# State read placed beside M of chunks 2 and 3: one change of TensorE's tiling less per batch

## The chip, the cores and the metric

One core of one Trainium2 chip. The time is device microseconds of one execution, from runs on the chip; the span is what the profile of the same execution shows from the first to the last instruction (1.7 to 2.1 us less in most runs, up to 3.0 in a few).

## The reference

A cross attention between tokens and a small state, in both directions, followed by a feed-forward layer over all rows of its result:

```python
B, H, S, Ns, D = (8, 8, 512, 32, 64)           # x: (B,H,S,D), state: (B,H,Ns,D)
a  = softmax(scale * x @ state.T);   xread = a  @ state
a2 = softmax(scale * state @ x.T);   sread = a2 @ x
attn = concatenate([xread, sread], axis=2)     # -> rows (B*(S+Ns), H*D = 512)
h = attn @ w_in                                # w_in: (512, 2048)
return (h / (1 + exp(-1.702 * h))) @ w_out     # w_out: (2048, 512)
```

(Shortened: the maxima and the 1e-9 of the softmax are left out.) All in 32-bit floats.

## The kernel before

The matmuls here write to PSUM, in banks; the program copies a bank out before it is written again. The token rows never form `xread`: the kernel multiplies the state into `w_in` first. That product is called M, per batch, in four chunks of 512 columns; `up` then multiplies M by the softmax weights. The state read `sread` is formed for all batches and goes through the layer at the end. `down` (the product with `w_out`) and, from batch 2 on, `up` use a Strassen scheme (fewer products of blocks, paid for with sums of blocks), hence the sums of M, which VectorE adds.

Each instruction of TensorE carries a size in the trace, 128*128 or smaller, called its tiling: eight matmuls of M, of tiling 64*32, start within 47 ns (360.820 to 360.867 us) and the next eight 453 ns after the first of them, while full-size matmuls of 128*128 start 216 ns apart. An "excursion" below is a way out of the full tiling and back. Three tilings occur: 128*128 for all large products and transposes, 64*32 for scores and M, 128*32 for the state read:

```python
psA = ctx.enter_context(tc.tile_pool(name="psA", bufs=2, space=bass.MemoryType.PSUM))  # tag "att"
psH = ctx.enter_context(tc.tile_pool(name="psH", bufs=2, space=bass.MemoryType.PSUM))  # tag "h"
...
def by_state(b, ps, rhs):                      # scores and M: 64 rows, 32 columns
    for j in range(NPR):
        for g in range(NG):
            rows, st = slice(D * g, D * (g + 1)), slice(Ns * j, Ns * (j + 1))
            nc.tensor.matmul(ps[g][st], A[b]["stT"][rows, st], rhs(rows, j), start=True, stop=True)

def att_M(b, c, spare=False):                  # two PSUM banks, from psH if spare, else psA
    ...
    by_state(b, ps, lambda rows, j: w_in[c][rows, j])
    for g in range(NG):
        nc.scalar.copy(m[:, g], ps[g])

def att_eT(b, g):                              # turns the states' softmax weights (128*128)
    ps = att_ps([P, SCH, P], f"eT_{b}_{g}")    # one bank of psA
    ...
    nc.scalar.copy(a["eT"][:, g], ps)

def att_sread(b):                              # 128 rows, 32 columns
    ps = att_ps([P, NG, D], f"sr_{b}")         # one bank of psA
    ...                                        # 32 matmuls of 64 columns
    nc.scalar.copy(sr, ps.rearrange("p g d -> p (g d)"))
```

Batches 2 to 7 are prepared while the batch ahead goes through `down`: after each block of eight large matmuls `product` runs what is in the next of 14 slots. The blocks are named by their PSUM bank: x in slots 0, 1, 4, 5; y in 2, 3, 6, 7, 10, 11; z in 8, 9, 12, 13.

```python
        at(5, att_scores, b)
        at(5, att_M, b, 0)
        at(5, att_M, b, 1, True)
        ...                                    # softmax in both directions, VectorE and ScalarE
        at(8, att_M, b, 2)
        at(8, att_M, b, 3, True)
        at(9, up_sums, b, 0)
        for g in range(NG):
            at(9 + g, att_eT, b, g)
        at(11, att_sread, b)
        at(11, up_sums, b, 1)
        at(12, att_srT, b)
        at(12, up_sums, b, 2)
```

A 32-bit matmul is two instructions in the trace and a transpose one (the four of an eT slot are x4), so a block of eight is 16, a chunk of M 16 and the state read 64.

Of the kernel before, what the change touches and what calls it, by code (L numbers as in the profile page):

```python
# [20 lines left out]
def kernel(  # L21
# [362 lines left out]
    def att_slots(b):  # L384

        slots = [[] for _ in range(14)]

        def at(i, fn, *args):
            slots[i].append((fn, args))

        at(0, att_state, b)
        for j in range(NPR):
            at(j, att_xT, b, j)
# [4 lines that stand above are left out]
        at(5, att_blocks, b)  # L398
        at(5, att_s_max, b)
        at(5, att_s_exp, b)  # L400
        at(5, att_x_exp, b)
        at(5, att_s_norm, b)
        at(5, att_x_norm, b)
        at(8, att_M, b, 2)
        at(8, att_M, b, 3, True)
        at(9, up_sums, b, 0)
        for g in range(NG):
            at(9 + g, att_eT, b, g)
        at(11, att_sread, b)
        at(11, up_sums, b, 1)  # L410
        at(12, att_srT, b)
        at(12, up_sums, b, 2)
        return slots

# [338 lines left out]
    for b in range(1, B):  # L753
        ahead = b + 1 < B
        if not ahead:
            for f in range(NF):
                up_s(f)
                if f > HF and f % 2:
                    s12("sr", (f - HF) // 2, B * Ns)
                    s3("sr", (f - HF) // 2, B * Ns)  # L760
            strassen("sr", B * Ns, lambda r, n: out_s[nb * r.start : nb * r.stop, :, n])
        slots = att_slots(b + 1) if ahead else [[]]
        if b > 1:
            slots[0].insert(0, (up_strassen(b), ()))
        strassen(b, S, lambda r, n: out_x[b, r, :, n].rearrange("r q n -> q r n"), slots)
        if b + 2 < B:
            load_state(b + 2)
            load_x(b + 2)
# [30 lines left out]
```

## Time and profile before

| | before |
|---|---|
| time, median of the first 3 runs | 756.31 us (755.9 to 757.17) |
| span of the profiled run | 755.7 us |
| TensorE busy | 743.6 us, 98% |
| one pass (from one batch's first transpose, stT, to the next one's) | 81.612 us |
| tilings entered in a pass | scores with M 0 and 1; M 2 and 3; state read |

The pass is what to look at. There are six, so five distances between them, and these agree within 3 ns. The prediction shows the chain of work and the weight loads of the third pass.

### The profile page before, as it was taken

To read this page: it belongs to the slowest core of one execution; us is meant where nothing else is said; L and a number is where in the kernel's file an instruction comes from. 1 tells how busy PE (TensorE), PEld (TensorE's weight loads), DVE (VectorE), ACT (ScalarE), POOL (GpSimd) and SP (SyncE) were. 2 spreads that over 40 slices of the span, in tenths; PEclk is the share of its full clock that TensorE was granted. 3 is DMA by queue.
4 is the path that set the end of the run, shared out by engine and by line. 5 is a ranking of instruction groups with operands and counts; after the bars stand their busy time and mean duration, and the time that the engine had idled before them with its cause. 6 is when DMAs were issued, how large, how long until landed. Compare 5 with 4: busy or idle time off the path is not lost.

```text
span 755.7 us, 9853 instructions
## 1 busy us (share of the span) xinstructions
PE 743.6 (98%) x4171; PEld 563.8 (75%) x4171; DVE 413.9 (55%) x712; ACT 231.7 (31%) x411; POOL 0.8 (0%) x8
## 2 busy tenths in 40 slices
PE   8989999999999999999999999999999999999997
PEld 3423454467888878887788788887888778888886
DVE  5999699632646373555637264638364550225511
ACT  4667611022324241433134232424142312104200
POOL 0000000000000000000000000000000000000000
PEclk9999999999999999999999999999999999999999
DMA  9811245010030000300030003000130000000001
GB/s 233 330 61 52 84 152 159 0 57 1 28 78 10 1 15 29 74 1 15 29 74 0 1 29 87 3 1 15 38 64 1 15 29 15 0 22 8 0 15 42
DMA packets 48763, 35.22 MB, mean 47 GB/s; under 512 B 36432, under 2 KB 44112, under 8 KB 48720
## 3 DMA queue, kind: packets, MB, share of 16 engines
q1 hardware_dynamic: 48720, 34.61, 15.9%
q8 instruction: 32, 0.52, 0.3%
q14 instruction: 11, 0.09, 0.0%
HBM read 25.69 MB, written 8.91 MB: 46 GB/s over the span
## 4 chain that ended last, share of the span: by engine, by line
PE 96%; SPq 2%; ACT 1%; DMA 1%; issue 0%; DVE 0%; ACTq 0%
PE y L494 19%; PE z L494 13%; PE x L494 13%; PE upy L578 8%; PE h L422 8%; PE o L447 7%; PE upx L578 5%; PE upz L578 5%; PE M L276 4%; PE h_sr L422 4%; PE xT L258 2%; PE y_sr L494 1%; SPq L131 1%; PE sr L371 1%; PE s L276 1%; PE z_sr L494 1%
## 5 line engine op out<-in xcount | busy, mean ns | idle before, releaser
L494 PE MATMUL x<-w_out,g 128*128 128x256 f32 x448 | 100.2, 379 | 0.0
L494 PEld LDWEIGHTS x<-w_out,g 128*128 128x128 f32 x448 | 84.2, 190 | 11.4 <-ACT osb L454 0.2
L587 DVE TENSOR_TENSOR g<-upy,g 128x512 f32<-128x512 f32 x72 | 48.1, 689 | 68.7 <-PE upy L578 68.7
L584 ACT ACTIVATE g<-g 128x512 f32<-128x512 f32 x72 | 44.8, 630 | 84.8 <-DVE g L587 84.8
L422 PE MATMUL h<-aT,M 128*128 128x512 f32 x128 | 59.9, 614 | 4.4 <-ACT M L351 4.4
L351 ACT COPY M<-M 128x512 f32<-128x512 f32 x64 | 33.2, 596 | 95.1 <-PE M L276 95.1
L422 PEld LDWEIGHTS h<-aT,M 128*128 128x128 f32 x128 | 24.2, 194 | 37.9 <-issue 25.5
L494 PE MATMUL z<-sums,later 128*128 128x256 f32 x224 | 51.1, 382 | 0.0
L494 PE MATMUL z<-w_out,g 128*128 128x256 f32 x224 | 50.8, 382 | 0.0
L494 PE MATMUL y<-sums,later 128*128 128x256 f32 x224 | 50.5, 379 | 0.0
L494 PE MATMUL y<-sums,g 128*128 128x256 f32 x224 | 50.5, 379 | 0.0
L494 PE MATMUL y<-w_out,g 128*128 128x256 f32 x224 | 50.1, 382 | 0.0
L494 PEld LDWEIGHTS y<-w_out,g 128*128 128x128 f32 x224 | 42.1, 190 | 10.5 <-issue 5.0
L494 PEld LDWEIGHTS z<-sums,later 128*128 128x128 f32 x224 | 42.1, 190 | 10.5 <-issue 5.0
L578 PE MATMUL upx<-aT,M 128*128 128x256 f32 x192 | 49.3, 379 | 0.0
L578 PE MATMUL upy<-ta,M 128*128 128x256 f32 x192 | 49.3, 379 | 0.0
L494 PEld LDWEIGHTS z<-w_out,g 128*128 128x128 f32 x224 | 41.6, 190 | 6.2
L494 PEld LDWEIGHTS y<-sums,g 128*128 128x128 f32 x224 | 41.6, 190 | 5.2
L494 PEld LDWEIGHTS y<-sums,later 128*128 128x128 f32 x224 | 41.6, 190 | 5.2
L471 DVE TENSOR_TENSOR later<-g,g 128x512 f32<-128x512 f32 (+1 forms) x32 | 20.8, 651 | 40.7 <-ACT g L425 40.7
L511 DVE TENSOR_TENSOR osb<-z,later 128x512 f32<-128x512 f32 x14 | 9.7, 692 | 60.2 <-PE z L494 60.2
L578 PEld LDWEIGHTS upx<-aT,M 128*128 128x128 f32 x192 | 36.5, 190 | 5.0
(130 smaller groups left out, 1023.0 us busy)
## 6 DMA issues: line engine op xcount, KB each, us to landing
later<-in_moe_w_out_dram SPq DMA_DIRECT2D x16, 512.0 KB
out_dram<-osb SPq DMA_DIRECT2D x32, 256.0 KB
xn<-in_x_dram SPq DMA_DIRECT2D x28, 256.0 KB
w_out<-in_moe_w_in_dram SPq DMA_DIRECT2D x12, 512.0 KB
later<-in_moe_w_in_dram SPq DMA_DIRECT2D x4, 512.0 KB
sums<-in_x_dram SPq DMA_DIRECT2D x4, 256.0 KB
stn<-in_state_dram SPq DMA_DIRECT2D x16, 32.0 KB
out_dram<-osb_sr SPq DMA_DIRECT2D x4, 128.0 KB
```

Source lines behind the costliest of these rows:

```text
L131: nc.sync.dma_start(xn[b][:, c], x_v[b, c])
L258: nc.tensor.transpose(ps[:, c], x_heads(b, c, j), ident)
L276: nc.tensor.matmul(ps[g][st], A[b]["stT"][rows, st], rhs(rows, j), start=True, stop=True)
L351: nc.scalar.copy(m[:, g], ps[g])
L422: nc.tensor.matmul(hps, lhs[i], rhs[i], start=(i == 0), stop=(i == n - 1))
L447: nc.tensor.matmul(ops, G[key, f // 2][:, f % 2, P * r : P * (r + 1)], w_out[:, f], start=(f == 0), stop=(f == NF - 1))
L471: nc.vector.tensor_tensor(out=s1, in0=a21, in1=a22, op=ALU.add)
L494: nc.tensor.matmul(ps[:, r], lhs[f][:, P * r : P * (r + 1)], rhs[:, f], start=(first and r == 0 and f == 0), stop=(f == HF - 1), skip_grou ...
L511: nc.vector.tensor_tensor(out=o, in0=ps, in1=with_, op=ALU.add)
L578: nc.tensor.matmul(ps[:, k], lhs[:, o : o + P], rhs, start=(first and k == 0), stop=True, skip_group_check=True)
L584: nc.scalar.activation(out=dst, in_=src, func=AF.Gelu_apprx_sigmoid)
L587: nc.vector.tensor_tensor(out=dst, in0=ps, in1=x, op=ALU.add)
```

## The change

The intent: sr (128*32) goes to the same slot as M of chunks 2 and 3 (64*32), so that TensorE leaves the full tiling twice in a pass and not three times. For that the weights must be turned earlier (slot 8), and M 2 and 3 go from slot 8 to 9, chunk 3 first. The whole diff:

```diff
-        at(8, att_M, b, 2)
-        at(8, att_M, b, 3, True)
-        at(9, up_sums, b, 0)
         for g in range(NG):
-            at(9 + g, att_eT, b, g)
-        at(11, att_sread, b)
+            at(8, att_eT, b, g)
+        at(9, att_sread, b)
+        at(9, att_M, b, 3, True)
+        at(9, att_M, b, 2)
+        at(10, up_sums, b, 0)
         at(11, up_sums, b, 1)
-        at(12, att_srT, b)
+        at(11, att_srT, b)
         at(12, up_sums, b, 2)
```

## The prediction

What no trace or run of this case shows is cut out of the recorded text, and the cuts are marked. The sum came to 686 ns a pass before and 491 after, a gain of 195 ns. What its terms were, in starts of single records: 92 = 308-216 into M, 23 = 453-430 in M's first group, 134 = 564-430 out of M, 104 = 320-216 in the first z matmul; for sr 93, 24 = 80-56, 112 = 168-56 and 104. What TensorE does in these nanoseconds is not shown. The 136 ns for the step from sr to M were an estimate from two of them, 112 out of sr and 24 for a small first group. The two rivals about tiling: before the runs no trace ruled either out. That weights are loaded beside a running matmul is shown inside a block: a z load starts 2 ns after the matmul before its own (363.020 and 363.018 us).

> **What bounds the kernel now.** I read the page's engine shares first, then the chain of work that ended last, then that chain again in a window of one batch, then the timelines of TensorE's matmuls and weight loads in that window, and last ScalarE and VectorE there, for the margins.
>
> The page says that TensorE is the bound and that nearly nothing interrupts it:
>
> ```profile
> PE 743.6 (98%) x4171; PEld 563.8 (75%) x4171; DVE 413.9 (55%) x712; ACT 231.7 (31%) x411; POOL 0.8 (0%) x8
> ...
> PE 96%; SPq 2%; ACT 1%; DMA 1%; issue 0%; DVE 0%; ACTq 0%
> ```
>
> So a nanosecond that TensorE gives back is a nanosecond of the kernel, and work on VectorE (55%) or ScalarE (31%) that only moves costs nothing unless TensorE comes to wait for it. The other TensorE figure, the weight loads, is 75%: they too have room.
>
> The change touches batches 2 to 7, which are prepared in slots between the blocks of matmuls of the batch ahead; six passes, all alike. Here is the chain (start us, us, what) over the middle of the third pass:
>
> ```profile
> 347.60 1.02 PE s L276 x16
> 348.62 1.72 PE M L276 x32
> 350.33 7.11 PE y L494 x32
> 357.44 3.45 PE z L494 x16
> 360.89 1.88 PE M L276 x32
> 362.77 3.65 PE z L494 x16
> 366.42 0.44 PE eT L360 x4
> 366.86 3.46 PE y L494 x16
> 370.31 0.44 PE eT L360 x4
> 370.75 3.46 PE y L494 x16
> 374.20 1.03 PE sr L371 x64
> 375.23 3.65 PE z L494 x16
> 378.88 0.11 PE srT L381
> 378.99 3.46 PE z L494 x16
> ```
>
> Each piece begins where the one before ends: TensorE alone, no wait. What the reader should see is that pieces of equal work differ. Sixteen full-size matmuls take 3.45 or 3.46 us, also beside transposes, but 3.65 after M and after sr. The 32 instructions of M take 1.72 us right after the scores (same tiling) but 1.88 us between full-size matmuls. These 0.16 and 0.20 us are the price of going into a tiling and coming back. The weight loads of the same stretch show where it lies (start, us, and in brackets the idle time before):
>
> ```profile
> 360.82 0.18 PEld L276 LDWEIGHTS M<-w_in,stT 64*32 64x32 f32 x16 [0.33 <-issue]
> ...
> 362.70 3.32 PEld L494 LDWEIGHTS z<-sums,later 128*128 128x128 f32 x16 [0.84 <-issue]
> ...
> 374.13 0.94 PEld L371 LDWEIGHTS sr<-xn,eT 128*32 128x32 f32 x64 [0.33 <-issue]
> 375.16 3.32 PEld L494 LDWEIGHTS z<-w_out,g 128*128 128x128 f32 x16
> ```
>
> Idle with no releaser ("issue") is 0.33 us before each first load of a new tiling: no semaphore explains it. Note also the tilings: M is 64*32, sr is 128*32, the rest 128*128. They are three, not two.
>
> [...]
>
> **The change, part by part.**
>
> *One change less, and its size.* From starts of single records, third pass. Into M: the last full matmul starts at 360.511, the first M load at 360.819, that is 308 ns later where a full matmul streams 216[...]; the first group of eight M matmuls then takes 453 ns to the second instead of 430, so 23 ns[...]. Out of M: last group at 362.132, first z load at 362.696, 564 ns less 430 is 134; the first z matmul then takes 320 ns to the second instead of 216, another 104[...]. Sum 92+23+134+104 = 353 ns, as the chain had it (0.16+0.20).
> For sr: into it 93, its first group of four 80 instead of 56 ns, so 24; out of it 168 less 56 is 112, then 104. Sum 333 ns.
> Before, these two excursions cost 353+333 = 686 ns in each pass. After, sr, M of chunk 3 and M of chunk 2 follow one another in one slot: in 93+24, from 128*32 to 64*32 once, out 134+104. No run before has that step from one small tiling to the other, so its price is my choice. [...] Sum 117+136+238 = 491 ns. **Gain 686-491 = 195 ns a pass**; in the chain's terms one return to full size (0.20 us) goes and both ways into small tilings stay.
>
> *Transposes of the states' weights.* Eight eT instructions leave two slots of four and stand together in slot 8. They are 109 ns apart and the blocks beside them are 3.45 to 3.46 either way: at most 5 ns, call it nothing.
>
> *Work moved.* The number of matmuls, loads, copies and VectorE operations is the same: the diff only moves calls. Sums of M (up_sums) and srT move by a slot on engines with room.
>
> *Sum.* 6 passes x 0.195 = 1.17 us. A pass is now 81.61 us (M begins at 279.28 and at 360.89) and should be 81.41. The tail, batches 0 and 1 and the output are untouched. 756.31 - 1.2 = **755.1 us**, -0.16%.
>
> **Will a new wait take its place?** Each margin, from the third pass:
> The weights e2 must be normalized before the transposes, now in slot 8 at 360.9. VectorE ends the last of these (L316) at 355.06+0.48 = 355.5. Margin 5.3 us; the other passes show the same to 0.1.
> eT must be copied (0.58 us each, L361) before sr: two copies end some 1.1 us after the transposes, and a block of 3.45 us lies between. Margin over 2 us.
> PSUM: the pool of two banks that eT, sr and M of chunk 2 share goes round. M of chunk 2's second bank is the one sr was in, so it waits for the copy of sr. That copy starts 0.29 us after the last sr group (375.015 to 375.30) and takes 0.27, so some 0.6 us. In between stands M of chunk 3, in the other pool: 0.14 us of change, then 0.45+0.43 us. Its bank is wanted after about 1.0 us. Margin 0.4 us, the thinnest; this is plainly why chunk 3 goes first.
> The sums need all four M copies (0.48 us apart, L351): done about 2.3 us after M, and the first product that needs a sum comes four blocks and more later. VectorE has about 4 us of sums (L554 to L556) and was idle 3.71 us just before them, waiting for the second eT transpose. That wait goes. It is off TensorE's path either way.
>
> **The rivals.**
> *The step between the small tilings is free.* [...] Then the pass gains 195+136 = 0.33 us, the whole 2.0 us: 754.3. For it: nothing in the trace. [...]
> *The step costs as much as going out and back in,*[...]. Then an additional 0.2 us, gain 0, 756.3. [...]
> *A wait for the sr copy.* If ScalarE comes late by 0.5 us (it shouldn't, it is 31% busy and idle 3.93 us ahead of that copy), the pass loses 0.1 us or more of its gain: 755.7 or above. The thin margin is for it.
> *A late eT or late sums.* Would cost 1 us or more a pass, 762 and above; margins of 2 to 5 us speak against.
>
> **Range and chances.** The middle is 755.1. The two tiling rivals span 754.3 to 756.3. The three runs before scatter from 755.9 to 757.17, so a median of a few runs can be off by 0.4. I take 754.2 to 756.1. A change of 2% is 15 us, ten times anything that I find on the path in either direction; faster 0.01, same 0.98, slower 0.01, the last for a stall not foreseen.
>
> **What would show it right or wrong.** In the changed kernel's chain: z in its second half 3.45 us after two eT groups; sr about 1.03; M about 1.86 us after it and not 1.72 (1.72 would mean a free step, over 2.0 a dear one or a wait); then y at 3.65; z after srT 3.46, not 3.65. The period should be 81.41. On weight loads, "issue" idle of 0.33 before sr stays, and the 0.84 us case appears once in this stretch, before y. A releaser "ACT sr" ahead of M would show the PSUM rival; "DVE e" or "ACT eT" ahead of eT or sr the late weights. The VectorE wait of 22.6 us of ms for eT should vanish without any effect on the time. I'd be wrong if the span falls by over 2 us or rises at all.

## The result, and the profile after

755.95 us (median of 4 runs, 754.79 to 757.03) against 756.2 (4 runs) of the kernel before; ratio 0.9994, 95% interval 0.9977 to 1.0012. A ratio here is the mean time of one kernel's runs over that of the other's of the same rounds, so not quite the ratio of the medians. By these times nothing is settled: the same within 2%, and the gain not clear of zero. The traces settle it. The spans of the profiled runs are 754.3 after and 755.7 before (mean granted clock 0.997 and 0.998), and a pass takes 81.412 us where it took 81.612.

The chain that ended last, third pass, kernel after (start us, us, engine, what, line, instructions):

```profile
347.00 1.02 PE s L276 x16
348.02 1.72 PE M L276 x32
349.74 7.11 PE y L494 x32
356.84 3.45 PE z L494 x16
360.30 0.87 PE eT L360 x8
361.17 3.46 PE z L494 x16
364.62 1.03 PE sr L371 x64
365.65 1.88 PE M L276 x32
367.53 7.11 PE y L494 x32
374.64 0.11 PE srT L381
374.75 6.91 PE z L494 x32
```

Put it beside the chain of before. M still takes 1.88 and sr still 1.03, so both ways *into* a small tiling are still paid. What went is one way back: the pieces that follow were 3.65+3.46+3.46 and 3.65+3.46, with two 0.2 us surcharges; now y is 7.11 (3.65+3.46) and z is 6.91, twice 3.46, with none.

The weight loads of the same pass (in brackets the idle time before, and the releaser, that is what the profile names as having ended it):

```profile
364.55 0.94 PEld L371 LDWEIGHTS sr<-xn,eT 128*32 128x32 f32 x64 [0.33 <-issue]
365.58 0.18 PEld L276 LDWEIGHTS M<-w_in,stT 64*32 64x32 f32 x16
...
367.46 6.77 PEld L494 LDWEIGHTS y<-sums,g 128*128 128x128 f32 x32 [0.84 <-DVE ta L548]
```

From sr to M the loads pause by 0.09 us (364.55+0.94 = 365.49, next 365.58), as they did from sr to z in the kernel before; the step is cheaper than that exit by what is lost in the first group after it (23 ns where the first z matmul loses 104), not by its pause. By starts of single records, the step between the tilings is this: last group of sr at 365.417, first M load at 365.583, which is 166 ns less the 56 of a group, 110; first group of M 453 ns where a later one takes 430, 23. **133 ns**, and the prediction took 136; from sr to z it had been 112+104 = 216.

The last line holds a lesson in reading. The pause before y is now put down to a VectorE operation on `ta`. But it is 0.84 us, to the digit what stood there as "issue" before, and the timeline of VectorE has the last operation on ta from 366.40 to 366.82, over half a microsecond ahead of the load. The name is the latest semaphore that the profile finds; what the pause holds is M's own work and the change: 0.28 us are the idle time that stands between any two groups of M's loads, 0.43 the last group of matmuls, and the rest, 0.13, is what the change adds.

No wait took the place of what was removed. The weights were ready 5.2 us before their transposes (L316 ends at 354.96, eT starts at 360.13), and sr's copy ended at 365.99 while the first group of M of chunk 2 starts at 366.468. VectorE's wait for the eT transposes (22.6 us in all) became a wait for ScalarE's copies of M (12.2 us), off the path.

### The profile page after: what moved, and what is told of

It reads as the page before. It is cut to its first block, busy times and chain, and to the rows that moved or that the text cites. A ratio compares the mean times of both kernels' runs of the same rounds, so it can differ in the third digit from the quotient of the medians.

```text
span 754.3 us, 9846 instructions
## 1 busy us (share of the span) xinstructions
PE 742.2 (98%) x4169; PEld 565.6 (75%) x4171; DVE 414.3 (55%) x712; ACT 231.1 (31%) x411; POOL 0.8 (0%) x8
## 4 chain that ended last, share of the span: by engine, by line
PE 96%; SPq 2%; ACT 1%; DMA 1%; issue 0%; DVE 0%; ACTq 0%
PE y L494 20%; PE z L494 13%; PE x L494 13%; PE upy L578 8%; PE h L422 8%; PE o L447 7%; PE upz L578 5%; PE upx L578 5%; PE M L276 4%; PE h_sr L422 4%; PE xT L258 2%; PE y_sr L494 1%; SPq L131 1%; PE sr L371 1%; PE s L276 1%; PE z_sr L494 1%
## 5 line engine op out<-in xcount | busy, mean ns | idle before, releaser
L578 PEld LDWEIGHTS upy<-ta,M 128*128 128x128 f32 x192 | 36.6, 190 | 4.9
```

The lines of the kernel that those rows point to most:

```text
L578: nc.tensor.matmul(ps[:, k], lhs[:, o : o + P], rhs, start=(first and k == 0), stop=True, skip_group_check=True)
```

## The experiments

Theory: each change of tiling has a price that the traces show, and the gain is one exit (sr's, 216 ns) plus one entry from the full tiling (117) less the step between the small ones (133), 0.2 us in each of six passes. Rivals: the earlier transposes or the ended VectorE wait give the gain; the order of chunks is indifferent; the price depends on the kind of step; and, for the times, the gain is chance.

### The change again, more runs

> The changed kernel as it is, timed in five rounds, because its first four runs scatter by 2.2 us and the effect is 1.2 us. Theory (one return to the full tiling less per pass, 0.198 us in each of six passes): ratio to before 0.998 to 0.999, centre 0.9984, and a pass from M to M of 81.41 us again. Rival (the 0.25 us between the medians is all there is, the profile's span fell by chance): the passes differ by less than 0.05 us from 81.61 in this profile, ratio 0.9997 or above.

Measured: 754.9 us (6 runs, 754.36 to 756.21) against 756.29 (11 runs, 755.77 to 758.22); ratio 0.9977, 95% interval 0.9962 to 0.9991. The passes are 81.412 us again, all five. The gain is real, and the ratio came out lower than expected for a reason that turns up further down.

### The state read put apart again

```diff
-        at(9, att_sread, b)
         at(9, att_M, b, 3, True)
...
-        at(11, att_srT, b)
+        at(11, att_sread, b)
+        at(12, att_srT, b)
```

> The changed kernel with only the state read put back in its old slot 11 (its transpose in 12): the states' weights are still turned early and M of chunks 2 and 3 is still one slot later, but the state read is not beside M. Theory (adjacency is the whole gain): a pass of 81.61 us as before, two pieces of 3.65 us or 7.11 us after two separate excursions, and the VectorE wait for the eT transposes gone without any use. Rival (turning the weights early, or ending VectorE's wait, gives part of the gain): a pass of 81.55 us or less.

Measured: passes of 81.610 us, the old value; 755.72 us (one run). The chain has the second exit back:

```profile
363.24 1.88 PE M L276 x32
365.11 7.10 PE y L494 x32
372.22 1.03 PE sr L371 x64
373.25 3.65 PE z L494 x16
```

Everything else of the change is in this kernel: early transposes, later M, no VectorE wait for eT. Together this is worth 2 ns. The adjacency is the whole gain.

### Chunk 2 ahead of chunk 3

```diff
+        at(9, att_M, b, 2)
         at(9, att_M, b, 3, True)
-        at(9, att_M, b, 2)
```

> The changed kernel with M of chunk 2 ahead of M of chunk 3. Theory (chunk 3 goes first because chunk 2's second bank is the one the state read has just used): TensorE waits for ScalarE's copy of sr, which ends some 0.6 us after the last group of sr where M would start after 0.17, so 0.45 us more, a pass of 81.85 us or so, 0.25 above the kernel before, and a wait of M for ACT sr in the views. Rival (the order is free, the copy is hidden): 81.41 us.

Measured: passes of 81.865 us, 0.453 more than the changed kernel and 0.253 more than the kernel before; 757.72 us (one run). The weight loads and, from ScalarE's timeline, the copy that they wait for:

```profile
365.15 0.14 PEld L276 LDWEIGHTS M<-w_in,stT 64*32 64x32 f32 x2
365.60 0.18 PEld L276 LDWEIGHTS M<-w_in,stT 64*32 64x32 f32 x15 [0.32 <-ACT sr L376]
```

```profile
365.29 0.27 ACT L376 COPY sr<-sr 128x128 f32<-128x128 f32 x1 [3.88 <-PE sr L371]
```

Here the releaser's name can be trusted: the copy ends at 365.56, the loads go on at 365.60, and there is no change of tiling between the two lines. Two instructions of the first bank start, then everything stands until the bank that sr was in is copied out. Two lines in the other order cost more than the whole change gains: the pool of two PSUM banks is why chunk 3 goes first.

### All of M beside the scores

If the price is per change, M's own excursion can go altogether: all four chunks beside the scores, the state read alone. PSUM allows it if the scores stand in the middle, which leaves time to copy the banks of chunks 0 and 1.

```diff
-        at(5, att_scores, b)
         at(5, att_M, b, 0)
         at(5, att_M, b, 1, True)
+        at(5, att_scores, b)
+        at(5, att_M, b, 2)
+        at(5, att_M, b, 3, True)
...
         at(9, att_sread, b)
-        at(9, att_M, b, 3, True)
-        at(9, att_M, b, 2)
```

> All four chunks of M beside the scores in slot 5 (0, 1, scores, 2, 3, so that PSUM banks are copied out in time), the state read alone in slot 9: one excursion for 64*32 and one for 128*32, no step between small tilings. Theory (the price is per change of tiling, 0.353 us for M's own way in and out): a pass of 81.61-0.35 = 81.26 us, 2.1 us less than before in all and 0.9 us less than the changed kernel, ratio 0.997. Rival (PSUM turns into the bound: chunk 2 waits for the copies of chunk 0 or chunk 3 for those of chunk 1; or the softmax, 1.7 us later, makes the eT transposes wait): a wait with releaser ACT M ahead of M, or DVE e ahead of eT, and a pass of 81.5 us or more.

Measured: passes of 81.251 us, 0.361 under the kernel before and 0.161 under the change (expected 81.26); 754.49 us (6 runs, 753.53 to 755.34) against the same 756.29; ratio 0.9968, 95% interval 0.9954 to 0.9981. The chain:

```profile
346.59 1.88 PE M L276 x32
348.47 0.86 PE s L276 x16
349.33 1.72 PE M L276 x32
351.04 7.10 PE y L494 x32
```

One 1.88, then 0.86 and 1.72 for the same kinds of work without an entry. Some loads of M do wait for ScalarE's copies (in the timeline 0.28 and 0.20 us idle), but these pauses lie beside running matmuls, and M keeps its 1.72. The later softmax costs nothing.

### The step the other way round

```diff
-        at(9, att_sread, b)
-        at(9, att_M, b, 3, True)
         at(9, att_M, b, 2)
+        at(9, att_M, b, 3, True)
+        at(9, att_sread, b)
```

The terms were those measured before, 134 ns on leaving M and 112 on leaving sr, 23 or 24 in a small first group and 104 in a full-size one.

> The changed kernel with the three reversed: M of chunk 2, M of chunk 3, then the state read, so the step between the small tilings goes from 64*32 to 128*32. Theory[...]: in 116, step 134+24, out 112+104, 490 ns in all where the changed kernel has 489: a pass of 81.41 us. Rival (the price hangs on the kind of step): another number. The copy of chunk 2's first bank ends only some 0.05 us before the state read wants that bank, so up to 0.1 us more with a releaser ACT M would be that wait and not the step.

Measured: passes of 81.412 us, equal to the change within 1 ns; 755.07 us (one run). The steps themselves are not equal. By starts of single records this one takes 158 ns: the last group of M starts at 364.723 and the first sr load at 365.287, 564 less 430 is 134; the first group of sr then takes 80 where a later one takes 56, 24. The other direction took 110+23. In either direction the step is an extra pause on leaving the old tiling (134 ns out of M, 110 out of sr) and the extra time of the first group in the new one (24 and 23), and since the way in and the way back swap these terms, the pass is the same. The wait for the bank that I allowed for didn't come, although a view names it:

```profile
365.29 0.94 PEld L371 LDWEIGHTS sr<-xn,eT 128*32 128x32 f32 x64 [0.84 <-ACT M L351]
```

0.84 us is what every exit from 64*32 shows between its last load and the next, with or without an ACT in its name, and the pass has no time in it for a wait.

### All of M beside the scores, in the plain order

```diff
-        at(5, att_M, b, 0)
-        at(5, att_M, b, 1, True)
         at(5, att_scores, b)
+        at(5, att_M, b, 0)
+        at(5, att_M, b, 1, True)
         at(5, att_M, b, 2)
```

> All of M in slot 5 as in the run before of that kind, but in the plain order: scores, chunks 0, 1, 2, 3. Theory (M of chunk 2 needs the banks of chunk 0, whose two copies end some 2.2 us after chunk 0 began, while TensorE is there after 1.7; chunk 3 the same for chunk 1): waits for ACT M of 0.5 to 0.7 us a pass, a pass of 81.75 to 81.95 us, so no better than the kernel before. Rival (order is free): 81.25 us.

Measured: passes of 82.015 us (the first 81.960), a bit beyond the expected 81.75 to 81.95; 760.22 us (one run). Two of its weight loads:

```profile
351.15 0.13 PEld L276 LDWEIGHTS M<-w_in,stT 64*32 64x32 f32 x2 [0.83 <-ACT M L351]
351.64 0.18 PEld L276 LDWEIGHTS M<-w_in,stT 64*32 64x32 f32 x14 [0.35 <-ACT M L351]
```

In the chain the four chunks of M take 4.20 us together where they would take 3.44 (two pairs at 1.72), so 0.76 of waiting. I had taken some 0.6; the four copies follow one another at 0.48 us, and chunk 3 waits too. Best and worst pass differ only by whether the scores come first or in the middle.

### Where the scatter comes from

The single runs of a kernel fell into two groups, told apart by the mean granted clock: 0.999 or 1.0, and 0.997 or 0.998. The traces of both kinds agree within 0.7 us up to 42 us. There a stretch of matmuls runs at half clock in four of the eight traces of kernels without zeros, for 3.41 us in each. From the table by stages (window us, length, PE busy, granted clock, DMA), first the profiled run of the kernel before, then that of the change in its second series:

```profile
40.00:43.00 3.00, 0.90 (x2) 0.99 0.00 0
43.00:46.00 3.00, 3.00 (x5) 0.50 0.01 3
```

```profile
40.00:43.00 3.00, 1.10 (x3) 1.00 0.00 0
43.00:46.00 3.00, 3.00 (x9) 1.00 0.01 3
```

Ahead of it TensorE sits idle for 2.12 us in both, waiting for ScalarE's first copies of M. Here it is in the kernel before, with 8.83 us for sixteen matmuls that take 7.13 in the other run:

```profile
42.10 8.83 PE L422 MATMUL h<-aT,M 128*128 128x512 f32 x16 [2.12 <-ACT M L351]
```

Afterwards the run with the half clock is 1.7 us behind. To test it, matmuls of zeros fill this gap and a later one, in the version with all of M beside the scores:

```diff
     att_M(1, 0)
+    keep_warm(6)
...
     att_M(0, 1)
+    keep_warm(4)
```

> All of M beside the scores as in the best run, and six and four matmuls of zeros in the two gaps (2.1 and 1.5 us) that TensorE has at 40 and 52 us, where it waits for ScalarE's first copies of M. Theory (the scatter of 2 us between fast runs is one stretch of 3.4 us at half clock, 42.8 to 46.2 us, that some runs have after the first of these gaps and others don't): no half clock there in the profile, all six runs within 0.5 us of each other at a granted clock of 0.999 or 1.0, spans near 751.9, time near 753.7, ratio to before 0.996. Rival (the half clock comes from something else): runs at 0.997 or 0.998 remain among the six.

Measured: 753.85 us (5 runs, 753.39 to 754.04) against 757.78 (9 runs); ratio 0.9955, 95% interval 0.9940 to 0.9969. They were run on another chip. All five at a clock of 0.999 or 1.0; they spread over 0.65 us, a little more than the 0.5 expected. The passes are 81.251 or 81.252 us, the gap is 0.71 us, and the stretch is at full clock:

```profile
40.00:43.00 3.00, 2.29 (x9) 1.00 0.00 0
43.00:46.00 3.00, 3.00 (x9) 1.00 0.01 3
```

```profile
41.90 7.13 PE L422 MATMUL h<-aT,M 128*128 128x512 f32 x16 [0.71 <-ACT M L351]
```

Both gaps were filled at once, but the half clock had begun at 42.67 to 43.41 us, ahead of the gap at 52, so that one can't have caused it.

Five such runs could be luck, so I put the zeros into the kernel before, and nothing else, and ran the best version again beside it.

> The kernel before with nothing but the six and four matmuls of zeros in the gaps at 40 and 52 us. Theory (they end the half clock of some runs and nothing else): every run at a granted clock of 0.999 or 1.0 with a span of 753.8 to 754.4 us, as the runs of the kernel before have it at that clock, passes of 81.61 us; of the plain kernel's runs beside it about half at 0.998 and 755.5 to 756.4. Rival (five runs of the best version without a half clock were luck, about 1 in 30 at even odds): some runs at 0.998.

> The best version once more, for more runs on another occasion. Theory: all at a clock of 0.999 or 1.0, spans of 751.5 to 752.4 us, 2.1 below the warmed kernel before of the same call, which is 6 passes x 0.36. Rival: as for the run beside it.

Measured: the kernel before with zeros 755.9 us (5 runs, spans 753.8 to 754.9; two of them 0.3 and 0.5 above what I expected, at a clock of 1.0, for a reason that I don't know), ratio 0.9986, 95% interval 0.9973 to 1.0; the best version 753.68 us (5 runs, spans 751.7 to 752.4, their median 2.1 below that of the other, as expected), ratio 0.9954, 95% interval 0.9941 to 0.9966; the plain kernel before 757.35 (9 runs). They were run on another chip. With the zeros none of 15 runs had the half clock; of the 29 runs of the plain kernel before in the three timed series, 16 had it (5 of 11, 6 of 9, 5 of 9). None of the 29 left a trace here, and three of the 15 did; the others are judged by their mean clock alone. Why some runs of one kernel have the half clock and others don't, no run shows.

That explains both ratios of the change. Sorted by clock, spans at 0.999 or above: before, 13 runs of the three timed series, mean 754.08; after, 7 runs of its two series, mean 752.89. The difference is **1.20 us**, against six passes of 0.200 = 1.20; within the second comparison alone (the change again, on one chip) it is 754.05 (6 runs) less 752.86 (5 runs), 1.19. At 0.998 or below: 755.89 (16 runs) and 754.63 (3 runs), difference 1.25. In the second comparison one of the changed kernel's six runs had the half clock and five of the other's eleven, so that the ratio lies below what the passes make it. In the first, two of the changed kernel's four had it; of the other's I know the clock of the profiled run alone, so there the same cause is likely and not shown.

### What didn't get to the chip

One excursion in a pass instead of two, by doing the state read of one batch beside the scores of the next, would need x and the turned weights for longer (8 KB and 4 KB more per partition by their shapes). By my account it didn't build for want of room, and what it would bring is not shown.

## Why the prediction was right

- **TensorE is the bound, and time given back there is time of the kernel.** Right: passes fell by 0.200 us and the spans, at equal clock, by 1.20.
- **The price of an excursion, 353 ns for M and 333 for sr.** Right: removing M's excursion altogether took 361 ns. The excursion of sr was never removed; its 333 is shown by starts of single records alone. (The first term of it, 93, is 91 when reckoned like M's 92, from the load; it stands before and after, so the gain is as it was.)
- **The step between small tilings, 136 ns by choice.** Right: 133 in the changed kernel; the reversed order, at 158 for its step, gives the same pass, as the same terms say. Both tiling rivals fall: a free step would have made the pass 81.28, a dear one 81.61.
- **The transposes and the moved work cost nothing.** Right: with them alone the pass is 81.610.
- **No new wait, the thinnest margin 0.4 us at sr's copy.** Right: 366.468 less 365.99 is 0.48, less 0.04 from copy to load 0.44, and with the chunks exchanged the wait appears with the size expected. I should add that this margin is that of the matmul; the load that goes with it was due at 366.04, just when the bank came free. Another margin was misread without harm: the copies of M end 1.3 us after M (366.76+2.05 against 367.53), not some 2.3.
- **The reading of the weight loads.** Not right as it stands. The idle 0.33 us stands before the first load of a *small* tiling only; before z it was 0.84 after M and 0.09 after sr, as the prediction's own lines show. Another reading, of whether a first load waits for the old tiling's end, is cut: it can't be seen. The first M load (360.819) starts 92 ns later than the usual 216 after the last full matmul, but 71 ns before that matmul's modelled end (360.511+0.379). The sums use neither.
- **Signs.** M after sr 1.88 (I wrote about 1.86), y with one surcharge, z without. VectorE's wait for eT vanished, but I didn't foresee that more than half of it would come back as a wait for M's copies.
- **The size.** 755.1 predicted, 755.95 measured. The gain of the sum was right; that the median fell into the range, 0.15 us below its upper end, was in part luck: two of the four runs had the half clock, which the prediction didn't know of, and the medians differ by 0.25 us where the passes make 1.20. I took the scatter as 0.4 us of a median without asking what it was. It is half a microsecond to two, in two groups, and larger than the effect.

## What to carry to other kernels

In this kernel a change of TensorE's tiling had a price by starts of single records (0.12 us into a small tiling, 0.13 or 0.16 from one to the other, 0.22 or 0.24 back), legible in the chain as the surcharge of equal pieces: put work of one tiling together first, and then unlike small tilings side by side, and check which PSUM bank each piece needs, since one bank wait (0.45 us here) outweighs several changes. Where an effect is smaller than the scatter of runs, measure a period that repeats inside the trace, and sort the runs by granted clock before comparing. An idle gap of TensorE like the one here, of 2.12 us, is worth filling with dummy matmuls for a trial, if what follows is on the path: by their mean clock 16 of 29 runs of the kernel that has it had the half clock, which left the traced run 1.7 us behind, and none of 15 with zeros in it (0.71 us left in the trace).
